# Attention norms with tokens on partitions, transposed back by DMA, in a linear-attention and PReLU feed-forward kernel

## The chip, the cores and the metric

The kernel runs on one core of a Trainium2 chip. The metric is the device time of one execution in microseconds, as the median of several runs. The core's engines work side by side, each through its own list of instructions in order: TensorE (PE; its weight loads are PEld), VectorE (DVE), ScalarE (ACT), GpSimd (POOL) and SyncE (SP). POOL and SP are used here almost only to issue DMAs: POOL the loads, SP the stores and the transposes.

## What is computed

There are 8 batches, 8 heads, 576 tokens and head dimension 64. Attention without a softmax is followed by an RMS norm over the head dimension and by a feed-forward layer with a parametric ReLU.

```python
kv = np.einsum('bhsd,bhse->bhde', k, v)
out = np.einsum('bhsd,bhde->bhse', q, kv)
rms = np.sqrt(np.mean(out * out, axis=-1, keepdims=True) + 1e-06)
attn = out / rms * g_norm                       # g_norm: 64 values
x = attn.transpose(0, 2, 1, 3).reshape(4608, 512)
h = x @ w_in                                    # 512 x 2048
g = np.maximum(h, 0.0) + alpha * np.minimum(h, 0.0)
y = g @ w_out                                   # 2048 x 512
```

Inputs and output are float32; the matmuls run in fp16 with float32 accumulation.

## The kernel before

The 4608 tokens are taken in nine windows of 512 (`W`). A batch has 576 tokens, so most windows hold the end of one batch and the start of the next. Heads are worked in four pairs, so that a pair fills 128 partitions.

**The feed-forward part.** For each window the hidden activations are made in 16 groups of 128 features. A group is `m1_group`: four matmuls of 512 columns (line 391) into a PSUM bank `h_ps`, then ACT makes `m_sb` = relu(-h) (line 398) and DVE combines both into `gt` (line 402), the fp16 activations. Two `m_sb` buffers are in use, and from window 2 on two PSUM banks for `h_ps` (`h_tags`). The second product of windows 1 to 8 is done by a Strassen-like scheme with seven products instead of eight, `prod_mm` (line 546), into three banks X, Y and Z; it needs sums of `gt` blocks (`s_sum`, DVE, lines 496 to 502) and reads of the banks (`y_read`: p1 and c11 on ACT, u2, u3, c22, c21 and c12 on DVE), after which rows are stored by SP. Window 0 takes the plain product (`y_mm`, line 416).

**The order** is written by hand. The main loop over `w` from 1 to 7 runs 16 units `u`. A unit issues group `u` of the first product of window `w`, then sums, then seven matmuls of the second product of window `w - 1` with its reads, and then a piece of the attention of window `w + 1`, by the tables `ATT_1` and `ATT_AT`. The last loop, over window 8's second product alone, has no attention and no first product.

**Attention.** For each pair: `step_t` (batches 0 to 2) turns q so that head dimension lies on partitions, with PE and a copy; from batch 3 (`B_NAT`) on `dma_t` does this with five DMA transposes on SP, all in unit 11. `step_kv` makes k^T v of a batch (five matmuls, line 327, and a DVE product with a block mask, line 335). `step_ot` multiplies it with the transposed q: `ot_ps` has the pair's features on partitions and 512 tokens as columns (line 349), and ACT squares it (line 355). `ssq_mm` sums the squares of a head over partitions by a matmul with a mask (line 365), and ACT makes `rstd` of it, 128 x 512 values (line 367). `norm` multiplies `ot_ps`, `g2col` (g_norm, one value a partition) and `rstd` into `xt` (DVE, line 375), the right-hand operand of the first product. No transpose of x is needed.

**Loads and buffers.** Weights stay in SBUF: `w_in_sb` in five parts, of 256, 256, 512, 512 and 512 features. k is regrouped by copies (DVE or ACT, `regroup`, lines 171 and 173). q has three buffers `qsb`, transposed q two (`qt_all`), and staging tiles two each. The pool for `ot_ps` has two banks.

Of the kernel before, what the change touches and what calls it, by code (L numbers as in the profile page):

```python
# [9 lines left out]
FP32 = mybir.dt.float32  # L10
# [7 lines left out]
def kernel(  # L18
# [29 lines left out]
    NC = D_MODEL // P  # L48
    assert NC == NPAIR and 0 < REM < P and P0 <= P and H % 4 == 0
    B_NAT = 3  # L50
    inv_d = 1.0 / D

    const_p = ctx.enter_context(tc.tile_pool(name="constp", bufs=1))
# [67 lines left out]
    bufs = []  # L121
    for i in range(NBUF):
        t = {}
        for nm in ("k", "v", "q"):
            n = 1 if nm == "v" else T0 if i == 0 else NT
            t[nm] = qkv_p.tile([P, n, H, D], FP16, name=f"{nm}sb{i}")
            if i > 0 or nm == "v":
                nc.vector.memset(t[nm][REM:P, n - 1, :, :], 0.0)
        bufs.append(t)
# [26 lines left out]
            )  # L156

    def buf_of(b, nm):
        return bufs[1 if nm == "q" and b >= B_NAT else b % NBUF][nm]

    def load_rem(b, nm):
        nc.gpsimd.dma_start(  # L162
# [2 lines left out]
        )  # L165

    def regroup(b, nm, h0, h1, eng=None):
        dst = bufs[b % NBUF][nm][:, 0:TPP, h0:h1, :].rearrange("p t h d -> p h t d")
        src = stages[b, nm][:, h0:h1, :, :]
        if eng is nc.scalar:  # L170
            nc.scalar.copy(out=dst, in_=src)
        else:
            (eng or nc.vector).tensor_copy(out=dst, in_=src)
# [35 lines left out]
    def load_w_in(i):  # L209
# [4 lines left out]
        )  # L214
        w_in_sb.append(t)

    def load_w_out(i):
        t = w_p.tile([P, GW, D_MODEL], FP16, name=f"w_out_sb{i}")
        nc.gpsimd.dma_start(
            out=t[:],  # L220
            in_=moe_w_out[i * GW * P : (i + 1) * GW * P, :].rearrange("(g p) m -> p g m", p=P),
        )
        w_out_sb.append(t)
# [25 lines left out]
    load_batch(1, ("v",))  # L249
    load_w_out(2)  # L250
    load_w_out(3)
    load_batch(2, ("q", "k", "v"))


    warm_ps = ps_q.tile([P, W], FP32, name="warm_ps", tag="q")
# [18 lines left out]
    def pair_cols(b, nm, j):  # L274
        def f(t):
            n = rows(b)
            if nm == "v" and b == 0:
                h = 2 * j % HH
                return stages[b, nm, 2 * j // HH][0:n, h : h + 2, t, :]
            if nm == "v" and t < TPP:  # L280
                return stages[b, nm][:, 2 * j : 2 * j + 2, t, :]
            if nm == "v":
                return bufs[b % NBUF][nm][0:n, 0, 2 * j : 2 * j + 2, :]
            return bufs[b % NBUF][nm][0:n, t, 2 * j : 2 * j + 2, :]
        return f

    def step_t(b, j, pool=(ps_s, "s")):
        qs = pair_cols(b, "q", j)
        qt_ps = pool[0].tile([P, n_runs(b) * rows(b)], FP16, name="qt_ps", tag=pool[1])
        c = 0  # L290
        for t in range(n_runs(b)):
            n = rows(b)
            nc.tensor.matmul(  # L293
                out=qt_ps[:, c : c + n],
                lhsT=qs(t),
                rhs=ident16[0:n, 0:n],
                is_transpose=True,
                start=(t == 0),
                stop=(t == n_runs(b) - 1),
            )  # L300
            c += n
        if j == 0:
            qt_all[b] = attn_p.tile([P, NPAIR, S], FP16, name="qt_all")
        qts[b, j] = qt_all[b][:, j, :]
        if b == 0 and j < 2:
            nc.vector.tensor_copy(out=qts[b, j], in_=qt_ps[:, 0:S])
        else:
            nc.scalar.copy(out=qts[b, j], in_=qt_ps[:, 0:S])

    qt_all = {}  # L310

    def dma_t(b):
        qt = attn_p.tile([P, NPAIR, S], FP16, name="qt_all")
        for t in range(NT):
            c0, c1 = t * P, min((t + 1) * P, S)
            src = stages[b, "q"][:, t] if t < TPP else buf_of(b, "q")[0:REM, TPP]
            nc.sync.dma_start_transpose(
                out=qt[:, :, c0:c1], in_=src.rearrange("p h d -> p (h d)"),
            )
        for j in range(NPAIR):  # L320
            qts[b, j] = qt[:, j, :]

    def step_kv(b, j, pool=(ps_s, "s")):
        ks, vs = pair_cols(b, "k", j), pair_cols(b, "v", j)
# [46 lines left out]

    def norm(w, j):
        ot_ps, rstd = ots.pop((w, j))
        xts[w, j] = xt_p.tile([P, W], FP16, name="xt", tag=f"xt{j}")
        nc.vector.scalar_tensor_tensor(  # L375
            out=xts[w, j][:], in0=ot_ps[:], scalar=g2col[:], in1=rstd[:],
            op0=ALU.mult, op1=ALU.mult,
        )

    gts = {}  # L380
# [8 lines left out]
    def m1_mm(h_ps, w, g, cs):  # L389
        for c in cs:  # L390
            nc.tensor.matmul(  # L391
                out=h_ps[:], lhsT=w_in_blk(c, g), rhs=xts[w, c][:],
                start=(c == 0), stop=(c == NC - 1),
            )

# [261 lines left out]
    ssq_mm(0, 2)  # L657
    keep_warm(1, warm_late)
    ssq_mm(0, 3, h_at(2))
    norm(0, 2)  # L660
    norm(0, 3)
    first = [ps_h.tile([P, W], FP32, name="h_ps", tag=f"h{g}") for g in range(3)]
    for c in range(3):
        for g in range(2):
            m1_mm(first[g], 0, g, (c,))
    m1_mm(first[2], 0, 2, (0, 1, 2))
    for g in range(3):
        m1_mm(first[g], 0, g, (3,))
        m1_evac(first[g], 0, g)
    h_turn[0] = 2  # L670
    for g in range(3, NF):
        m1_group(0, g, {3: S_POOL, 4: O_POOL, 5: O_POOL, 6: Q_POOL}.get(g))
        if g == 14:
            regroup(1, "k", 0, H)
            nc.vector.memset(bufs[0]["k"][REM:P, TPP, :, :], 0.0)


    ys = {}
# [82 lines left out]
            ATT_1.setdefault(at, []).append((what, j))  # L761
    ATT = {"t": step_t, "kv": step_kv, "ot": step_ot, "ssq": step_ssq}

    def attention(w, u):
        if w < NW:
            for what, j in (ATT_1 if w == 2 else ATT_AT).get(u, ()):
                if what == "t" and w >= B_NAT:
                    continue
                if w < B or what in ("ot", "ssq"):
                    if w == 2 and what in ("kv", "ssq"):  # L770
                        pool = Q_POOL if j % 2 == 0 else S_POOL
                        (step_kv if what == "kv" else step_ssq)(w, j, pool)
                    else:
                        ATT[what](w, j)

    REG_AT = {8 + 2 * j: (("k", j),) for j in range(NPAIR)}

    Y3_AT = [(8, 8), (8, 8), (8, 8), (8, 9), (9, 9), (9, 10), (10, 10), (10, 10), (10, 11), (11, 11), (11, 12), (12, 12), (12, 13), (13, 14), (14, 15), (15, 16)]
    REG_2 = {2 * j: (("k", j),) for j in range(NPAIR)}

    for w in range(1, NW):
        if w + 2 < B:
            load_gated(w + 2)
        for u in range(NF):
# [2 lines left out]
                unit_sums(w, u)  # L787
            if w == 1 and u == 2:
                regroup(2, "k", 0, H)
            if w == 1 and u == 3:  # L790
                dma_t(3)
            if w == 2 and u == 0:
                h_tags[0] = ("h1", "h2")
            if w > 2 and u == 0:
                y_read(w - 2, "c12")
            if w == 1:
# [4 lines left out]
            else:  # L801
                for i in range(u * PER, (u + 1) * PER):
                    prod_mm(w - 1, *Y_LIST[i])
                for what in Y_READS.get(u, ()):
                    y_read(w - 1, what)
            attention(w + 1, u)
            if w == 1:
                for k in {5: (0,), 7: (1,)}.get(u, ()):
                    s_sum(1, 1, k)
                    s_sum(1, 2, k)  # L810
            if w + 2 < B:
                for nm, j in REG_AT.get(u, ()) if w > 1 else ():
                    regroup_pair(w + 2, nm, j)
                if u == 11 and w > 1:
                    dma_t(w + 2)
            if w == 2:
                for nm, j in REG_2.get(u, ()):
# [51 lines left out]
```

## Time and profile before

Three runs took 283.4, 283.55 and 284.07 us; the median is 283.55. The profiled execution took 283.02 us, and its span from the first to the last instruction is 281.3 us. The clock granted to PE was 1.0 of full speed.

| Row of the profile | count | us each | us in all |
|---|---|---|---|
| first product, matmul, L391 | 576 | 0.379 | 145.4 |
| gt, DVE, L402 | 144 | 0.746 | 106.9 |
| m_sb, ACT, L398 | 144 | 0.598 | 85.9 |
| xt (norm), DVE, L375 | 36 | 0.744 | 26.6 |
| rstd, ACT, L367 | 36 | 0.689 | 24.6 |
| squares, ACT, L355 | 36 | 0.598 | 21.2 |
| sum of squares, matmul, L365 | 36 | 0.379 | 13.6 |
| ot, matmul, L349 | 64 | 0.286 | 13.6 |

The count is that of instructions. "us each" runs from start to end of one instruction; those of PE and also those of DVE and ACT overlap a little with their successors, so the pitch from start to start is shorter, and "us in all" counts overlapping time once. Group lines of the profile name the source line, the engine, the operation, output and inputs, and the idle time of the engine just before, with what ended it. Rows of busy times give a stretch in us from the span's start, its length, then the busy time and the count of instructions for PE, PEld, DVE, ACT and POOL, the PE clock, the share of DMA and GB/s.

### The profile page before, as it was taken

What the parts mean: (1) busy time and instruction counts of PE and PEld (TensorE: products, weight loads), DVE (VectorE), ACT (ScalarE), POOL (GpSimd) and SP (SyncE); (2) the same over time, 40 slices, a digit from 0 to 9 for tenths busy, and PEclk for the clock granted to TensorE, in tenths of its full rate; (3) what the DMA queues carried; (4) which work ended last, traced back from release to release, by engine and by line L of the source; (5) the groups of instructions that cost most, each with busy time, mean ns of one, the idle gap of its engine ahead of it and who ended that gap; (6) DMA issues with size and microseconds to landing.
All of it is one profiled execution on the core that took longest, in us unless ns stands there. A gap on an engine that the chain in (4) does not pass through costs nothing.

```text
span 281.3 us, 4978 instructions
## 1 busy us (share of the span) xinstructions
PE 273.9 (97%) x1888; PEld 173.6 (62%) x1888; DVE 219.8 (78%) x418; ACT 156.9 (56%) x268; POOL 61.8 (22%) x85
## 2 busy tenths in 40 slices
PE   7899999999999999999999999999999999999995
PEld 3444544554666676666666666666666666666784
DVE  6669729897778877887879787978887788787872
ACT  3567447697676645764576466645554566443310
POOL 8843333740630046006300450000000000000000
PEclk9999999999999999999999999999999999999999
DMA  8999999999794389946963698330112011201223
GB/s 164 198 207 195 198 201 193 192 136 143 100 170 85 93 84 150 165 112 115 158 102 97 121 150 123 93 106 1 40 37 75 2 37 37 77 0 37 77 76 114
DMA packets 77628, 31.37 MB, mean 112 GB/s; under 512 B 45780, under 2 KB 77284, under 8 KB 77604
## 3 DMA queue, kind: packets, MB, share of 16 engines
q0 software_dynamic: 55600, 18.85, 58.8%
q1 hardware_dynamic: 21108, 11.25, 16.1%
q10 hardware_dynamic: 896, 0.95, 1.0%
q8 instruction: 15, 0.25, 0.3%
q14 instruction: 9, 0.07, 0.1%
HBM read 36.71 MB, written 9.44 MB: 164 GB/s over the span
## 4 chain that ended last, share of the span: by engine, by line
PE 84%; DMA 10%; POOL 3%; issue 1%; DVE 1%; ACT 0%; DVEq 0%; POOLq 0%
PE h_ps L391 39%; PE yY L546 15%; PE yZ L546 10%; PE yX L546 10%; DMA vst<-in_v_dram 5%; DMA w_in_sb<-in_moe_w_in_dram 5%; PE kv_ps L327 3%; PE ot_ps L349 3%; PE ssq_ps L365 2%; PE y L416 2%; POOL w_in_sb L212 1%; POOL vst L136 1%; POOL kst L136 0%; PE qt_ps L293 0%; POOL qst L136 0%
## 5 line engine op out<-in xcount | busy, mean ns | idle before, releaser
L391 PE MATMUL h_ps<-xt,w_in_sb 128*128 128x512 f16 x576 | 145.4, 379 | 0.7 <-DVE gt L402 0.5
L402 DVE SCALAR_TENSOR_TENSOR gt<-m_sb,beta_sb,h_ps 128x512 f16<-128x512 f32 x144 | 106.9, 746 | 40.8 <-ACT m_sb L398 39.0
L398 ACT ACTIVATE m_sb<-h_ps 128x512 f32<-128x512 f32 x144 | 85.9, 598 | 75.8 <-PE h_ps L391 61.1
L391 PEld LDWEIGHTS <-w_in_sb 128*128 128x128 f16 x576 | 54.8, 98 | 47.0 <-issue 1.7
L546 PEld LDWEIGHTS <-s 128*128 128x128 f16 x512 | 50.1, 98 | 19.3
L546 PEld LDWEIGHTS <-gt 128*128 128x128 f16 x384 | 37.6, 98 | 15.1 <-issue 0.4
L546 PE MATMUL yY<-wsum,s 128*128 128x256 f16 x256 | 36.3, 273 | 0.0
L546 PE MATMUL yX<-w_out_sb,gt 128*128 128x256 f16 x256 | 35.1, 273 | 0.1
L355 ACT ACTIVATE sq_sb<-ot_ps 128x512 f16<-128x512 f32 x36 | 21.2, 598 | 16.5 <-PE ot_ps L349 16.4
L367 ACT ACTIVATE rstd<-ssq_ps,eps_t 128x512 f32<-128x512 f32 x36 | 24.6, 689 | 9.7 <-PE ssq_ps L365 9.2
L375 DVE SCALAR_TENSOR_TENSOR xt<-ot_ps,g2col,rstd 128x512 f16<-128x512 f32 x36 | 26.6, 744 | 3.2 <-ACT rstd L367 3.2
L162 POOL DMA_DIRECT2D qsb<-in_q_dram x7 | 4.9, 695 | 79.1 <-DMA qt_all<-qsb 77.0
L153 POOL DMA_DIRECT2D qst<-in_q_dram x20 | 17.7, 920 | 1.9 <-DVE gt L402 1.9
L546 PE MATMUL yZ<-w_out_sb,s 128*128 128x256 f16 x128 | 17.6, 273 | 0.0
L546 PE MATMUL yZ<-wsum,s 128*128 128x256 f16 x128 | 17.6, 273 | 0.0
L546 PE MATMUL yY<-wsum,gt 128*128 128x256 f16 x128 | 17.6, 273 | 0.0
L416 PE MATMUL y<-w_out_sb,gt 128*128 128x512 f16 x64 | 17.0, 379 | 0.5 <-DMA w_out_sb<-in_moe_w_out_dram 0.5
L349 PE MATMUL ot_ps<-qt_all,kv_sb 128*128 128x512 f16 (+7 forms) x64 | 13.6, 286 | 0.4 <-DVE kv_sb L335 0.3
L498 DVE TENSOR_TENSOR s<-s,gt 128x512 f16<-128x512 f16 x32 | 13.5, 421 | 0.5
L327 PEld LDWEIGHTS <-ksb 128*128 128x128 f16 (+1 forms) x164 | 11.4, 98 | 3.7 <-DVE ksb L193 1.1
L365 PE MATMUL ssq_ps<-sq_sb,mask 128*128 128x512 f16 x36 | 13.6, 379 | 0.1
L335 DVE TENSOR_TENSOR kv_sb<-kv_ps,mask 128x128 f16<-128x128 f32 x32 | 9.1, 286 | 5.5 <-PE kv_ps L327 5.5
(66 smaller groups left out, 210.1 us busy)
## 6 DMA issues: line engine op xcount, KB each, us to landing
out_dram<-y_sb SPq DMA_DIRECT2D x19, 256.0 KB, 2.2
kst<-in_k_dram POOLq DMA_DIRECT2D x7, 512.0 KB, 8.6
vst<-in_v_dram POOLq DMA_DIRECT2D x7, 512.0 KB, 11.0
qst<-in_q_dram POOLq DMA_DIRECT2D x20, 128.0 KB, 6.8
w_out_sb<-in_moe_w_out_dram POOLq DMA_DIRECT2D x4, 512.0 KB, 16.0
out_dram<-y_sb SPq DMA_DIRECT2D x25, 64.0 KB, 3.5
w_in_sb<-in_moe_w_in_dram POOLq DMA_DIRECT2D x3, 512.0 KB, 11.3
out_dram<-y_sb SPq DMA_DIRECT2D x9, 128.0 KB, 2.1
```

Of the source, the lines that this page charges most:

```text
L153: nc.gpsimd.dma_start(out=st[:, t, :, :], in_=srcs["q"][b, :, t * P : (t + 1) * P, :].rearrange("h p d -> p h d"),)
L327: nc.tensor.matmul(out=kv_ps[:], lhsT=ks(t), rhs=vs(t), start=(t == 0), stop=(t == n_runs(b) - 1),)
L349: nc.tensor.matmul(out=ot_ps[:, n0 - w * W : n1 - w * W], lhsT=kvs[b, j][:], rhs=qts[b, j][:, n0 - b * S : n1 - b * S], start=True, stop=True,
L355: nc.scalar.activation(out=sq[:], in_=ot_ps[:], func=AF.Square)
L365: nc.tensor.matmul(out=ssq_ps[:], lhsT=mask16[:], rhs=sq[:], start=True, stop=True)
L367: nc.scalar.activation(out=rstd[:], in_=ssq_ps[:], func=AF.Abs_reciprocal_sqrt, bias=eps_t[:], scale=inv_d,)
L375: nc.vector.scalar_tensor_tensor(out=xts[w, j][:], in0=ot_ps[:], scalar=g2col[:], in1=rstd[:], op0=ALU.mult, op1=ALU.mult,)
L391: nc.tensor.matmul(out=h_ps[:], lhsT=w_in_blk(c, g), rhs=xts[w, c][:], start=(c == 0), stop=(c == NC - 1),)
L398: nc.scalar.activation(out=m_sb[:], in_=h_ps[:], func=AF.Relu, scale=-1.0)
L402: nc.vector.scalar_tensor_tensor(out=gts[w, i][:, r, :], in0=m_sb[:], scalar=beta_sb[:, g : g + 1], in1=h_ps[:], op0=ALU.mult, op1=ALU.add,)
L416: nc.tensor.matmul(out=y[:], lhsT=gt_cols(w, g, a * P, (a + 1) * P), rhs=w_out_blk(g), start=(g == 0), stop=(g == NF - 1),)
L546: nc.tensor.matmul(out=bank, lhsT=lhs, rhs=rhs, start=fresh, stop=(c == NK - 1), skip_group_check=True,)
```

## The change

From window 4 on (`W_ROW`) attention is made with tokens on partitions. `rows_mm` takes 128 tokens at a time: the transposed q is the stationary operand and k^T v the moving one, a 128-column matmul for each pair, into one bank of 128 tokens x 512 features. Where the 128 tokens straddle two batches, two matmuls add up, each with 64 columns of zeros beside its q; for this the transposed q lies in two fixed tiles `qt_sb` with zeroed pads. ACT squares the bank, DVE sums the squares of each head by a reduce along the free dimension (128 x 8 results), ACT makes `rstd_r` of these, and DVE multiplies the bank by `rstd_r`, broadcast along the head, into `x_rows`. A DMA transpose on SP then writes these 128 tokens into `xt`, now one tile for all four pairs. `ssq_mm` and `norm` stay for windows 0 to 3.

g_norm is no longer part of the norm: the five parts of `w_in_sb` are multiplied by `g2col` in place on DVE in the stage of window 0. From batch 5 on the transposes of q are issued in portions in units 9, 10 and 11; those of batch 3 move from unit 3 to unit 12 of the loop over window 1, those of batch 4 from unit 11 to unit 12. q has two buffers instead of three. k^T v of windows 4 to 7 moves to units 0 to 3. Two entries of `Y3_AT`, which places the last row block of window 0's second product, and a bank turn at the start of window 2 change too.

```diff
-        for nm in ("k", "v", "q"):
+        for nm in ("k", "v", "q") if i < 2 else ("k", "v"):
...
     def buf_of(b, nm):
-        return bufs[1 if nm == "q" and b >= B_NAT else b % NBUF][nm]
+        return bufs[min(b, B_NAT) % 2 if nm == "q" else b % NBUF][nm]
...
+    def scale_w_in(i):
+        nc.vector.tensor_scalar(
+            out=w_in_sb[i][:], in0=w_in_sb[i][:], scalar1=g2col[:], scalar2=None, op0=ALU.mult,
+        )
...
+    PAD = P // 2
+    qt_sb = [const_p.tile([P, NPAIR, PAD + S + PAD], FP16, name=f"qt_sb{i}") for i in range(2)]
+
+    def dma_t(b, ts=tuple(range(NT))):
+        qt = qt_sb[b % 2][:, :, PAD : PAD + S]
+        for t in ts:
...
     def norm(w, j):
         ot_ps, rstd = ots.pop((w, j))
-        xts[w, j] = xt_p.tile([P, W], FP16, name="xt", tag=f"xt{j}")
-        nc.vector.scalar_tensor_tensor(
-            out=xts[w, j][:], in0=ot_ps[:], scalar=g2col[:], in1=rstd[:],
-            op0=ALU.mult, op1=ALU.mult,
+        nc.vector.tensor_mul(out=xt_cols(w, j), in0=ot_ps[:], in1=rstd[:])
...
+    def rows_mm(w, i):
+        n0 = w * W + i * P
+        b, r = divmod(n0, S)
+        o_ps = ps_o.tile([P, W], FP32, name="or_ps", tag="o")
+        for j in range(NPAIR):
+            cols = o_ps[:, j * P : (j + 1) * P]
+            if r + P <= S:
+                c = PAD + r
+                nc.tensor.matmul(
+                    out=cols, lhsT=qt_sb[b % 2][:, j, c : c + P], rhs=kvs[b, j][:],
+                    start=True, stop=True,
+                )
+            else:
...
+        sq = attn_p.tile([P, W], FP16, name="sq_sb")
+        nc.scalar.activation(out=sq[:], in_=o_ps[:], func=AF.Square)
+        ots[w, "r", i] = (o_ps, sq)
+
+    def rows_ssq(w, i):
+        o_ps, sq = ots.pop((w, "r", i))
+        ssq = attn_p.tile([P, H], FP32, name="ssq_r")
+        nc.vector.tensor_reduce(
+            out=ssq[:], in_=sq[:].rearrange("p (h d) -> p h d", h=H),
+            axis=mybir.AxisListType.X, op=ALU.add,
+        )
+        rstd = attn_p.tile([P, H], FP32, name="rstd_r")
+        nc.scalar.activation(
+            out=rstd[:], in_=ssq[:], func=AF.Abs_reciprocal_sqrt, bias=eps_t[:], scale=inv_d,
+        )
+        ots[w, "r", i] = (o_ps, rstd)
+
+    def rows_norm(w, i):
+        o_ps, rstd = ots.pop((w, "r", i))
+        xr = attn_p.tile([P, H, D], FP16, name="x_rows")
+        nc.vector.tensor_tensor(
+            out=xr[:], in0=o_ps[:].rearrange("p (h d) -> p h d", h=H),
+            in1=rstd[:].unsqueeze(2).to_broadcast([P, H, D]), op=ALU.mult,
+        )
+        xt_cols(w, 0)
+        nc.sync.dma_start_transpose(
+            out=xts[w][:, :, i * P : (i + 1) * P], in_=xr[:].rearrange("p h d -> p (h d)"),
+        )
...
+    scale_w_in(0)
     norm(0, 2)
     norm(0, 3)
...
+    scale_w_in(1)
     m1_mm(first[2], 0, 2, (0, 1, 2))
...
+    SCALE_AT = {3: 2, 7: 3, 11: 4}
     h_turn[0] = 2
     for g in range(3, NF):
+        if g in SCALE_AT:
+            scale_w_in(SCALE_AT[g])
         m1_group(0, g, {3: S_POOL, 4: O_POOL, 5: O_POOL, 6: Q_POOL}.get(g))
         if g == 14:
             regroup(1, "k", 0, H)
-            nc.vector.memset(bufs[0]["k"][REM:P, TPP, :, :], 0.0)
+            for nm in ("k", "q"):
+                nc.vector.memset(bufs[0][nm][REM:P, TPP, :, :], 0.0)
+            for t in qt_sb:
+                nc.vector.memset(t[:, :, 0:PAD], 0.0)
+                nc.vector.memset(t[:, :, PAD + S : PAD + S + PAD], 0.0)
...
+    ATT_ROW = {}
+    for what, ats in (("kv", (0, 1, 2, 3)), ("mm", (4, 6, 8, 10)), ("ssq", (5, 7, 9, 11)), ("norm", (6, 8, 10, 12))):
+        for j, at in enumerate(ats):
+            ATT_ROW.setdefault(at, []).append((what, j))
+    ROWS = {"kv": step_kv, "mm": rows_mm, "ssq": rows_ssq, "norm": rows_norm}
+    QT_AT = {9: (0, 1), 10: (2,), 11: (3, 4)}
+
     def attention(w, u):
-        if w < NW:
+        if W_ROW <= w < NW:
+            for what, j in ATT_ROW.get(u, ()):
+                if what != "kv" or w < B:
+                    ROWS[what](w, j)
+            if w + 1 < B:
+                dma_t(w + 1, QT_AT.get(u, ()))
+        elif w < NW:
...
-            if w == 1 and u == 3:
-                dma_t(3)
             if w == 2 and u == 0:
                 h_tags[0] = ("h1", "h2")
+                h_turn[0] = 1
...
+            if w == 1 and u == 12:
+                dma_t(3)
...
-                if u == 11 and w > 1:
+                if u == 12 and 1 < w < W_ROW - 1:
                     dma_t(w + 2)
```

## The prediction

> **What bounds the kernel now.** I read the page first (busy shares, clock, chain), then a window's row of busy times, then the timelines of TensorE, VectorE (DVE) and ScalarE (ACT) over one window, then the start, and last the tile of the transposed q for its DMAs.
>
> ```profile
> PE 273.9 (97%) x1888; PEld 173.6 (62%) x1888; DVE 219.8 (78%) x418; ACT 156.9 (56%) x268; POOL 61.8 (22%) x85
> PE 84%; DMA 10%; POOL 3%; issue 1%; DVE 1%; ACT 0%; DVEq 0%; POOLq 0%
> 155.70:184.60 28.90, 28.90 (x211) 19.34 (x209) 23.65 (x45) 17.38 (x31) 7.33 (x9) 1.00 0.89 121
> ```
>
> TensorE bounds it: the chain runs through PE for 84%, and in a window of 28.90 us PE is busy for 28.90. So PE work that goes is worth its full length, if nothing else becomes late. Within one unit of that window:
>
> ```profile
> 162.68 0.39 PE L327 MATMUL kv_ps<-vst,ksb 128*128 128x128 f16 x4
> 162.91 0.22 PE L327 MATMUL kv_ps<-vsb,ksb 128*128 128x128 f16 x1
> 162.96 1.03 PE L391 MATMUL h_ps<-xt,w_in_sb 128*128 128x512 f16 x4
> 163.83 0.93 PE L546 MATMUL yX<-w_out_sb,gt 128*128 128x256 f16 x7
> 164.59 0.38 PE L365 MATMUL ssq_ps<-sq_sb,mask 128*128 128x512 f16 x1
> 164.81 1.03 PE L391 MATMUL h_ps<-xt,w_in_sb 128*128 128x512 f16 x4
> ...
> 164.03 0.60 ACT L398 ACTIVATE m_sb<-h_ps 128x512 f32<-128x512 f32 x1 [1.31 <-DVE kv_sb L335]
> 165.01 0.69 ACT L367 ACTIVATE rstd<-ssq_ps,eps_t 128x512 f32<-128x512 f32 x1 [0.38 <-PE ssq_ps L365]
> 165.87 0.60 ACT L398 ACTIVATE m_sb<-h_ps 128x512 f32<-128x512 f32 x1 [0.18 <-PE h_ps L391]
> ...
> 164.66 0.75 DVE L402 SCALAR_TENSOR_TENSOR gt<-m_sb,beta_sb,h_ps 128x512 f16<-128x512 f32 x1 [0.62 <-ACT m_sb L398]
> 165.32 0.68 DVE L568 TENSOR_TENSOR u<-yY,p 128x512 f32<-128x512 f32 x1
> 165.92 0.74 DVE L375 SCALAR_TENSOR_TENSOR xt<-ot_ps,g2col,rstd 128x512 f16<-128x512 f32 x1
> 166.58 0.74 DVE L402 SCALAR_TENSOR_TENSOR gt<-m_sb,beta_sb,h_ps 128x512 f16<-128x512 f32 x1
> ```
>
> Starts give the real pitches. PE: a 512-column matmul 0.216 us, five 128-column ones 162.68 to 162.96, so 0.056 each, seven of the second product 0.76; a bare unit is 0.87 + 0.76 = 1.63. The third group is ACT, the fourth DVE. From the start of a group (162.96) it is 1.07 us to m_sb and 1.70 to gt. A group may only start when gt of two groups before has left its bank (two banks), 2.50 us after that group started (1.70 + 0.75 + 0.05); two units are 3.26 or more. So DVE may run about 0.8 us late, no more. On ACT, rstd waits for PE only, so the next m_sb is never held by DVE. That is what changes.
>
> [...] No reduce is in this trace; the 128x2048 fp16 copy[...] took 686. [...] the trace has 685 for `u`. [...] the trace has 689 for rstd at N = 512[...].
>
> **The change, part by part.**
>
> *PE work, windows 4 to 8.* Per window go four ssq matmuls (4 x 0.216) and the ot ones (4 x 0.22): 1.74. Sixteen 128-column matmuls come: 16 x 0.056 = 0.90. That saves 0.84 a window, 4.2 in five; windows 5 and 7 have a block that straddles two batches (4 more each, 0.45 in all): 3.8 saved.
>
> *DVE and ACT, same windows.* In the built order, at units 5, 7, 9 and 11 DVE has gt(u), the other sums of that unit, then the reduce; ACT has m_sb(u), then rstd_r, which waits for that reduce, then m_sb(u+1); and the next thing in DVE's list is gt(u+1), which waits for m_sb(u+1). So DVE idles through reduce -> rstd_r -> m_sb -> gt, four times a window. From the reduce's start to gt(u+1): reduce 0.69[...], hand-over DVE to ACT 0.09 (at 19.27 m_sb follows a gt that ended at 19.18), rstd_r 0.28 - 0.09 = 0.19[...], m_sb to gt 0.63 (164.03 to 164.66): 1.60.
>
> Now DVE in order, from the start of group 5 as 0, with pitches from the timeline: gt 0.66, u and c reads 0.60, x_rows 0.60 (a PSUM tensor_tensor like `u`), sums 0.34 (0.45 before a dependent one). gt(5) 1.70; u2 2.36; reduce 2.96; gt(6) 4.56; two sums 5.22; x_rows 6.01; gt(7) 6.61; sum 7.27; reduce 7.61; gt(8) 9.21; sum 9.87; x_rows 10.21; gt(9) 10.81; sum 11.47; u3 11.81; reduce 12.41; gt(10) 14.01; sum 14.67; x_rows 15.01; gt(11) 15.61; sum 16.27; c22 16.61; reduce 17.21; gt(12) 18.81; sum 19.47; x_rows 19.81, done 20.50.
>
> PE needs gt(u) + 0.80 for group u+2: group 8 at 5.36 (0.25 late), 9 at 7.41 (0.20), 10 at 10.01 (0.97), 11 in time, 12 at 14.81 (1.32), 13 in time, 14 at 19.61 (1.54). Together 4.28 a window; without lateness group 14 would start at 9 x 1.63 + 3 x 0.22 = 15.33. Five windows: 21.4.
>
> *SP and the transposes of x.*
>
> ```profile
> L317 SPq DMA_TRANSPOSE qt_all<-qst x20: 1191/1217/1840, 62.9 to 182.0; - x20
> DMA to landing us min/median/max: 2.3/2.3/7.1
> ```
>
> One transpose holds SP for about 1.25 us with its gap and lands 2.3 after issue. The last x_rows is done at 20.50, the next window's first group is due at 19.61 + 2 x 1.63 = 22.87 and needs all four transposes. With SP free, 20.55 + 2.3 is just in time. In the loops over windows 3 to 5, SP works through what was queued ahead: third x transpose 15.75, one of q, the c22 store (0.5), two of q, so the last is issued about 21.4 and lands about 23.7: 0.8 late, three times, 2.4. Bounds: 0, and 4.8 more each if the 7.1 us landing is met. Stores behind them have four y buffers: nothing waits. The q portions' loads are in long before; POOL's order of loads is unchanged, and moving block 3's transposes to unit 12 costs nothing, since before they only started at 62.9, when q had landed.
>
> *w_in scaled in window 0.* DVE row of the start:
>
> ```profile
> 15.50 1.41 DVE L375 SCALAR_TENSOR_TENSOR xt<-ot_ps,g2col,rstd 128x512 f16<-128x512 f32 x2 [1.11 <-ACT rstd L367]
> 18.43 7.29 DVE L402 SCALAR_TENSOR_TENSOR gt<-m_sb,beta_sb,h_ps 128x512 f16<-128x512 f32 x10 [1.52 <-ACT m_sb L398]
> ```
>
> The first scaling fits the 1.11 idle. The second follows the norms (done about 17.2), where group 2 would start at 16.44: gt(0) moves by 0.5, to 18.95. The third stands behind gt(2) (pitch 0.73: 20.4, free 21.1) and takes 0.69: group 4, which waits for it, starts at 21.85. Before it started at 19.1 (m_sb of group 10 at 25.36, less 1.07, less 6 x 0.864): +2.75. The fourth stands behind gt(6): from group 4, 2 x 0.864 + 1.70 + 0.66 + 0.69 + 0.05 = 4.83, where four groups take 3.45: +1.38; the fifth the same. Sum 5.5.[...] Five more memsets (0.27 for q's buffer, four pads of about 0.2 by the 0.17 to 0.27 of the ones in the trace: 1.1 us) stand before gt(15), so that the fourth row block of y, which takes its bank, waits 0.75. Two DMA waits of PE in this stretch (0.46 and 0.38) go, as the data are there by then. Net +5.4.
>
> *At nothing:* the norm without g (0.06 x 16 on DVE, under PE), the merged xt tile, kv in units 0 to 3 (0.1 at one of them).
>
> **Sum.** 283.02 (the profiled execution; span 281.3, 1.7 around it; median of the runs 283.55) + 21.4 + 2.4 + 5.4 - 3.8 = 308.4. I say 308.
>
> **Rivals.**
> 1. *The PE saving decides* (the faster side): DVE finds cover for reduces and scalings, and 3.8 us go: 279.2. For it: DVE is idle for a fifth of the window, and adding 4 x (0.6 + 0.6 - 0.66) = 2.2 leaves it under 28. Against: the idle time lies between gt and m_sb, and the new chain uses it up in order. It decides if reduce to gt took under 0.55 instead of 1.60 (20 bubbles), and w_in were scaled ahead of need.
> 2. *Only window 0 pays:* 283.0 + 5.4 - 3.8 = 284.6. For it: the scaling is as certain as anything here; against, as in 1.
> 3. *Half of the window loss:* the reduce at 0.53, rstd_r at 0.1 and some sums out of the way: 1.35 instead of 1.60 takes 1.0 a window away and the transposes' lateness: 301; with more cover still, 290 to 300.
> 4. *The transposes queue up* (over 4 us to land): 312 to 318.
>
> **How the numbers follow.** Forecast, 301 to 313: 0.70. Rival 3 under 301: 0.11. Rival 4: 0.07. Rival 2: 0.04. Rival 1: 0.08. What can be told from no change is about 0.3%, 0.9 us. Range 296 to 314; it leaves out rivals 1 and 2, the lower part of 3 and the upper of 4. Faster 0.08, same 0.02, slower 0.90.
>
> **What would show it.** Right: PE below 0.9 busy in the slices of windows 4 to 8, the PE wait for DVE gt (0.5 us now) grown to some 20; ACT rstd_r waiting for the DVE reduce, 20 times; a loop over windows 3 to 5 near 33 us instead of 28.9; PE waiting for w_in from DVE three times before 35 us. Wrong: windows near 28.1 with PE full, or a reduce far under 0.5.

## The result, and the profile after

The changed kernel took 312.97 us in the median of four runs (312.39 to 314.14), beside 283.48 (283.1 to 284.07) for the kernel before on the same chip: 1.105 times as long, with a 95% interval of 1.102 to 1.108. The forecast was 308, with a range of 296 to 314; the median lies near its upper end. The profiled execution took 314.14 us with a span of 312.2, so 30.9 more than the span before.

From the page of the changed kernel: busy time of each engine, two rows of the span in 40 slices, and the chain of what ended last.

```profile
PE 277.1 (89%) x1920; PEld 173.3 (55%) x1920; DVE 231.7 (74%) x447; ACT 144.2 (46%) x268; POOL 61.8 (20%) x85
...
PE   7868899998999998779977898689888987899995
...
PEclk9998999999999999999999999999999999999999
...
PE 66%; DMA 13%; DVE 11%; ACT 4%; issue 2%; POOL 2%; ACTq 0%; DVEq 0%; POOLq 0%
```

PE was busy for 97% of the span; now it is for 89%. The row of slices shows where it went: a 6 at the start, then nearly full slices, then 7s and 8s and a 6 among the 9s from slice 16 to 35 (a slice is 7.8 us), which are the loops over windows 3 to 7, in which attention for windows 4 to 8 is made. The share of PE in the chain fell from 84% to 66%; DVE (1% to 11%), ACT (0% to 4%) and DMA (10% to 13%) took it.

From the waits of the changed kernel (what waited, for what; us in all, times, longest):

```profile
ACT rstd_r L419 <- DVE ssq_r L414: 48.9, 20, 3.1
...
PE h_ps L447 <- DVE gt L458: 15.8, 16, 1.3
...
PE h_ps L447 <- DMA xt<-x_rows: 5.6, 4, 2.0
PE h_ps L447 <- DVE w_in_sb L219: 5.5, 4, 2.3
```

PE's three waits in these lines are 26.9 us, of a loss of 30.9. On ACT, rstd_r waits 20 times for the reduce, once for each block of rows; on PE, the first product waits for gt in the same windows, for the transposes of x at four loop starts, and for the scaled weights at the start.

The chain that the prediction worked out, seen in the loop over window 4 (timeline of DVE and ACT; start, length, what it waited for in brackets):

```profile
150.98 0.68 DVE L414 TENSOR_REDUCE ssq_r<-sq_sb 128x8 f32<-128x512 f16 x1
...
151.69 0.30 ACT L419 ACTIVATE rstd_r<-ssq_r,eps_t 128x8 f32<-128x8 f32 x1 [2.01 <-DVE ssq_r L414]
151.90 0.58 ACT L454 ACTIVATE m_sb<-h_ps 128x512 f32<-128x512 f32 x1
...
152.51 0.75 DVE L458 SCALAR_TENSOR_TENSOR gt<-m_sb,beta_sb,h_ps 128x512 f16<-128x512 f32 x1 [0.85 <-ACT m_sb L454]
```

ACT stands for 2.01 us in front of rstd_r. For the last 1.0 of these the next group's m_sb could have run behind it, since the matmuls that it reads ended at 150.68; then m_sb runs, and only then can DVE go on with gt. From the start of the reduce to the start of gt it is 1.53 us, four times a window.

The timeline of PE at the start, the first three of its waits for scaled weights:

```profile
17.63 2.33 PE L447 MATMUL h_ps<-xt,w_in_sb 128*128 128x512 f16 x10 [0.40 <-DVE w_in_sb L219]
22.30 5.21 PE L447 MATMUL h_ps<-xt,w_in_sb 128*128 128x512 f16 x16 [2.34 <-DVE w_in_sb L219]
28.79 3.63 PE L447 MATMUL h_ps<-xt,w_in_sb 128*128 128x512 f16 x16 [1.27 <-DVE w_in_sb L219]
```

Sixteen matmuls take 5.21 us after the second wait and 3.63 after the third. The windows of the same stretch say why (us; busy time and count for PE, PEld, DVE, ACT, POOL; then the granted clock):

```profile
22.30:25.00 2.70, 2.70 (x7) 1.04 (x8) 0.74 (x2) 0.60 (x1) 0.81 (x1) 0.50 1.52 192
25.00:28.80 3.80, 2.53 (x12) 0.85 (x10) 2.83 (x5) 1.79 (x3) 1.55 (x3) 0.93 1.41 198
```

The clock is 0.50 in the first 2.7 us after the wait of 2.34 and, by the 0.93 of the next row, for some 0.5 us more. The sixteen matmuls lose 1.6 us by it, which no step of the prediction had.

To compare kernels I read two times off each PE timeline: when the first product of loop 2 (the loop over window 2) starts, and how long it is from there to the start of the last group of the first product. The first holds the start, the second the loops.

| Kernel | time (one profiled execution) | loop 2 starts at | from there to the last group |
|---|---|---|---|
| before | 283.02 | 66.51 | 197.50 |
| after | 314.14 | 72.80 | 221.93 |
| 1: rstd behind the next m_sb | 301.06 | 71.62 | 210.03 |
| 2: q transposes behind those of x | 306.28 | 70.66 | 216.21 |
| 3: no scaling of w_in | 310.39 | 66.02 | 224.96 |
| 3b: no scaling, q of batch 3 loaded last | 305.90 | 66.03 | 220.59 |
| 4: no row windows | 290.43 | 73.91 | 197.51 |
| 5: short reduce | 309.55 | 72.81 | 217.32 |
| 6: 2 and 5 together | 300.17 | 73.09 | 207.66 |
| 7a: 1, 2 and early scaling | 290.44 | 66.96 | 204.09 |
| 7b: 7a, rows and q transposes two units earlier | 291.28 | 66.78 | 205.09 |
| 8: 7b, four x_rows buffers and more | 280.70 | 66.53 | 194.89 |

So of the 30.9 us, 6.3 are lost before loop 2, 24.4 in the loops and 0.2 after them. The row of 7b is one of its three slower executions (291.28 to 295.13 us, with a granted clock of 0.987 to 0.994); the other three, at about 1.0, have a median of 287.43.

The times also hold what PE's clock did. Wherever it fell before PE's last matmul, it stayed at 0.50 for some 3.4 us (read from rows of busy times over 0.2 us each; in the changed kernel from 22.14 to 25.55). Such a stretch costs up to 1.7 us, as an estimate from these two numbers: half its length. It fell once at the start in the changed kernel and in 4, 5 and 6, and in the loops twice in 1, once in 3 and in 7b, and for 6.8 and 3.4 us in 5. It did not fall in the kernel before, in 2, 3b, 7a and 8. The mean granted clock goes with this: 0.995 in the changed kernel, 0.994 in 4, 6 and 7b, 0.993 in 3, 0.988 in 1 and 0.976 in 5, and at least 0.998 in the others. Experiments 1 to 6 are single executions, so a difference of 2 or 3 us between them can be the clock's alone.

### The profile page after: what moved, and what is told of

Read it like the earlier page. It is cut to its first block, busy times and chain, and to the rows that moved or that the text cites. A ratio compares the mean times of both kernels' runs of the same rounds, so it can differ in the third digit from the quotient of the medians.

```text
span 312.2 us, 5142 instructions
## 1 busy us (share of the span) xinstructions
PE 277.1 (89%) x1920; PEld 173.3 (55%) x1920; DVE 231.7 (74%) x447; ACT 144.2 (46%) x268; POOL 61.8 (20%) x85
## 4 chain that ended last, share of the span: by engine, by line
PE 66%; DMA 13%; DVE 11%; ACT 4%; issue 2%; POOL 2%; ACTq 0%; DVEq 0%; POOLq 0%
PE h_ps L447 31%; PE yY L602 12%; PE yX L602 8%; DMA vst<-in_v_dram 6%; DMA xt<-x_rows 6%; DVE gt L458 6%; PE yZ L602 5%; ACT m_sb L454 4%; PE y L472 3%; PE kv_ps L331 3%; PE or_ps L393 1%; POOL qst L154 1%; DVE x_rows L427 1%; PE ot_ps L353 1%; DVE w_in_sb L219 1%
## 5 line engine op out<-in xcount | busy, mean ns | idle before, releaser
L447 PE MATMUL h_ps<-xt,w_in_sb 128*128 128x512 f16 x576 | 147.3, 382 | 27.3 <-DVE gt L458 15.8
L447 PEld LDWEIGHTS <-w_in_sb 128*128 128x128 f16 x576 | 54.1, 98 | 77.3 <-issue 27.5
L602 PEld LDWEIGHTS <-gt 128*128 128x128 f16 x384 | 37.5, 98 | 14.9
L419 ACT ACTIVATE rstd_r<-ssq_r,eps_t 128x8 f32<-128x8 f32 x20 | 6.0, 301 | 48.9 <-DVE ssq_r L414 48.9
L427 DVE TENSOR_TENSOR x_rows<-or_ps,rstd_r 128x512 f16<-128x512 f32 x20 | 13.7, 684 | 0.5 <-DMA xt<-x_rows 0.5
L331 PE MATMUL kv_ps<-vst,ksb 128*128 128x128 f16 (+1 forms) x136 | 12.6, 219 | 1.6 <-DMA vst<-in_v_dram 1.4
L414 DVE TENSOR_REDUCE ssq_r<-sq_sb 128x8 f32<-128x512 f16 x20 | 13.6, 678 | 0.0
L552 DVE TENSOR_TENSOR s<-gt 128x512 f16<-128x512 f16 x32 | 13.3, 419 | 0.1
## 6 DMA issues: line engine op xcount, KB each, us to landing
w_out_sb<-in_moe_w_out_dram POOLq DMA_DIRECT2D x4, 512.0 KB, 15.8
```

Of the source, the lines that this page charges most:

```text
L331: nc.tensor.matmul(out=kv_ps[:], lhsT=ks(t), rhs=vs(t), start=(t == 0), stop=(t == n_runs(b) - 1),)
L414: nc.vector.tensor_reduce(out=ssq[:], in_=sq[:].rearrange("p (h d) -> p h d", h=H), axis=mybir.AxisListType.X, op=ALU.add,)
L427: nc.vector.tensor_tensor(out=xr[:], in0=o_ps[:].rearrange("p (h d) -> p h d", h=H), in1=rstd[:].unsqueeze(2).to_broadcast([P, H, D]), op= ...
L447: nc.tensor.matmul(out=h_ps[:], lhsT=w_in_blk(c, g), rhs=xts[w][:, c, :], start=(c == 0), stop=(c == NC - 1),)
L552: nc.vector.tensor_add(out=t[:], in0=a21, in1=a22)
L602: nc.tensor.matmul(out=bank, lhsT=lhs, rhs=rhs, start=fresh, stop=(c == NK - 1), skip_group_check=True,)
```

## The experiments

Theory A is the prediction's: DVE and ACT wait for each other in their orders (reduce, rstd_r, m_sb, gt), and that, not the amount of work, makes PE wait. Theory SP: the transposes of x come late because q's stand ahead of them in SP's list. The rivals were that the duration of the work on DVE decides, and that the start pays for most of it. Beside the experiments the kernel before took 283.31, 283.37 and 283.33 us.

**1. rstd_r issued behind the next group's m_sb.** The computation is the same.

```diff
+        ots[w, "r", i] = (o_ps, ssq)
+
+    def rows_rstd(w, i):
+        o_ps, ssq = ots.pop((w, "r", i))
         rstd = attn_p.tile([P, H], FP32, name="rstd_r")
...
-    for what, ats in (("kv", (0, 1, 2, 3)), ("mm", (4, 6, 8, 10)), ("ssq", (5, 7, 9, 11)), ("norm", (6, 8, 10, 12))):
+    for what, ats in (("rstd", (6, 8, 10, 12)), ("kv", (0, 1, 2, 3)), ("mm", (4, 6, 8, 10)), ("ssq", (5, 7, 9, 11)), ("norm", (6, 8, 10, 12))):
```

> Only change to the changed kernel: rstd_r of a row block is issued on ScalarE after the next unit's m_sb instead of before it; same instructions, same count. Theory A (the hand-over reduce, rstd_r, m_sb, gt stalls VectorE in order): from the reduce's start to the next gt 0.6 us instead of 1.53, 20 times, so some 3.7 us a window off VectorE's list; most of PE's 15.8 us of waits for gt goes; about 296 us (293 to 300). Theory B (VectorE simply has too much work with reduce and x_rows): the list is no shorter, within 3 us of 313. Theory C (the DMA transposes of x are the main cost): also within 3 us of 313, and the PE waits for xt stay near 5.6.

301.06 us. The timeline of DVE and ACT around one reduce:

```profile
181.79 0.67 DVE L414 TENSOR_REDUCE ssq_r<-sq_sb 128x8 f32<-128x512 f16 x1
182.39 0.73 DVE L462 SCALAR_TENSOR_TENSOR gt<-m_sb,beta_sb,h_ps 128x512 f16<-128x512 f32 x1
```

gt now follows the reduce at once, 0.60 after its start instead of 1.53. PE's wait for gt fell from 15.8 to 2.6 us. So the chain is shown to be the cause of these waits, with no work taken away. But the gain stopped 5 us short of the expected 296. The waits of this kernel, and the row of PE's clock from its page:

```profile
PE h_ps L451 <- DMA xt<-x_rows: 7.8, 4, 2.6
PE h_ps L451 <- DVE gt L462: 2.6, 5, 1.3
...
PEclk9999999999999999997999799999999999999999
```

The wait for the transposes of x grew from 5.6 to 7.8: the loops became shorter, and the transposes did not come earlier by as much. After the two longest of these waits (2.55 and 2.35 us, before loops 4 and 5) the clock fell to half, the two 7s of the row, which is worth up to 3.4 us more.

**2. q's transposes behind those of x.**

```diff
-    QT_AT = {9: (0, 1), 10: (2,), 11: (3, 4)}
+    QT_AT = {13: (0, 1), 14: (2,), 15: (3, 4)}
```

> Only change: the five transposes of q are issued in units 13 to 15, behind all four of x, instead of 9 to 11. Theory A with SP's queue as a second cost: the waits of the first group of a window for xt fall in the loops over windows 3, 4 and 5 (1.8, 2.0 and 1.2 us now) to about the 0.8 that the loop over window 7 has without q transposes; 309 to 311 us. Theory C (transposes dominate): 304 or less. If the landing itself is late whatever stands ahead of it: no change, 313.

306.28 us, 3 to 5 better than expected, though not the 304 of theory C. The wait for xt fell from 5.6 to 0.8 us and that for gt stayed at 15.8, as SP had it. By the table 5.7 us were won in the loops. Another 2.1 lie before loop 2, which the edit doesn't touch: in this run the wait of 2.31 us for the weights was followed by sixteen matmuls in 3.63 us, at full clock.

**3. No scaling of w_in.** This leaves out the multiplication by g_norm.

```diff
-    scale_w_in(0)
...
-    scale_w_in(1)
...
-        if g in SCALE_AT:
-            scale_w_in(SCALE_AT[g])
```

> Leaves out the five multiplications of w_in by g_norm, so g_norm is not applied at all; everything else as in the changed kernel. If the waits for the scaled w_in and the halved PE clock after the longest of them make the start late: the loop over window 1 starts about 6.2 us earlier (0.5 of the 7.15 is gt of group 15 behind the memsets), 306 to 307 us, and the PE clock stays at 1.0 from 20 to 29 us. If the data would be late anyway, as w_in's loads: less than 2 us.

310.39 us: a miss. Loop 2 starts at 66.02, so the start is regained in full, 6.8 us; but loop 2 then takes 35.57 us, where it takes 29.75 in the kernel before. Of these 5.8 us, 4.0 are one wait in PE's timeline, and behind it the clock was at half from 75.6 to 79.0, worth some 1.7 more:

```profile
74.28 0.38 PE L331 MATMUL kv_ps<-vst,ksb 128*128 128x128 f16 x4 [3.97 <-DMA vst<-in_v_dram]
```

v of batch 3 is issued at 58.99, within half a microsecond of when it was before, and takes 15.2 us to land instead of 11.4. On SP, in this kernel and below in the kernel before:

```profile
56.73 8.01 SPq L321 DMA_TRANSPOSE qt_sb<-qst  x4
```

```profile
62.92 5.37 SPq L317 DMA_TRANSPOSE qt_all<-qst  x4
```

Before, the transposes of q of batch 3 began 4.4 us behind the load of v; here they begin 2.3 ahead of it and run beside it. In the changed kernel they begin 1.4 ahead (62.42 and 63.80), v takes 14.3 us, and PE waits 1.0 for it. That gave theory T.

**3b. As 3, with q of batch 3 loaded behind its v**, so that its transposes can't run beside that load.

```diff
-        if b == B_NAT:
-            load_q(b)
         load_rem(b, "k")
...
         load_main(b, "v")
+        if b == B_NAT:
+            load_q(b)
```

> Leaves out the scaling of w_in by g_norm, as the third experiment did, and loads q of batch 3 after its v instead of ahead of its k. Theory T (the q transposes of batch 3 no longer wait for the old buffer, start 6 us earlier and run beside the load of v, which then lands late): v lands in about 10 us instead of 15.2, kv of batch 3 waits for it less than 1 us instead of 3.97, and the time is 306 to 307.5. Theory L (the load of v is late for another reason, such as the weights' loads or chance): the wait stays above 3 and the time at 310. If q itself is then late, the wait shows at the first product of loop 2 or at ot of batch 3 as a wait for qt_sb.

305.90 us. v of batch 3 took 8.8 us to land, q's transposes start at 65.03, behind it, and PE's wait for v is 0.4. Loop 2 takes 29.76 again. That is as T has it. The landing of this load goes with the start of the transposes: 15.2 us where they begin 2.3 ahead of it, 14.3 at 1.4 ahead, 11.4 at 4.4 behind, 8.8 with none beside it. Against the 312.97 of the changed kernel the run is 7.1 us faster, of which 6.8 lie at the start; in loop 2 the wait of 1.0 for v has gone too. Note what happened in 3: work was taken away, an engine came free, transfers started earlier, and they collided with others.

**4. No row windows**, with the scaling and the new q buffers kept.

```diff
-    W_ROW = 4
+    W_ROW = 9
```

> Only change: no window takes the row path (it would start at window 9, and there are windows 0 to 8); w_in scaled, buffers, moved transposes as in the changed kernel. Computes the same. If the row windows cost 23 and the start 7: 290 to 291 us, windows of 28.9 us with PE full. If the merged xt tile, the two q buffers or the moved transposes of blocks 3 and 4 had a cost of their own, it would show here as more than 292.

290.43 us, as expected. The loops take 197.51 us, those before 197.50. All that is left, 7.1 us, is the start (7.4 by the table, 1.0 of it a wait for v at 8.2 us that is 0.4 in the changed kernel). So the cost of the change is two separate things, 7 at the start and the rest in the row windows.

**5. A reduce over 8 of the 64 elements of a head.** This leaves out 7/8 of the squares.

```diff
-            out=ssq[:], in_=sq[:].rearrange("p (h d) -> p h d", h=H),
+            out=ssq[:], in_=sq[:].rearrange("p (h d) -> p h d", h=H)[:, :, 0:8],
```

> Leaves out 7/8 of the squares: the reduce sums only 8 of the 64 of each head, so that it takes some 0.2 instead of 0.68 us; the wait for rstd_r stays as it is. Theory A (the sum of VectorE's work between two gt decides, reduce, hand-over and wait together): each of the 20 reduces gives its 0.48 us back wherever VectorE is late, at most 9.6 us in all, less where a group had slack: 303 to 306 us, PE's wait for gt from 15.8 to 6 to 9. Theory W (the engines' waiting on each other decides, the reduce itself lies in idle time): 310 us or more, the wait for gt above 13.

309.55 us, which is between the two. (In this expectation and the next, A stands for the whole way from reduce to gt, with the reduce itself.) The reduce takes 0.21 us instead of 0.68, and the wait for gt fell from 15.8 to 7.8, inside A's 6 to 9. The time did not follow: the wait for xt rose to 7.5 us, its longest to 3.15, and after the two longest (3.15 and 2.21) PE's clock fell again (after the first, four matmuls took 1.86 us instead of 1.02). By the lengths of these stretches, less 0.9 us in which PE stood anyway, the clock cost some 4.7 us in the loops; without it the run would be at about 305, inside A's 303 to 306. That is an estimate. Alone, this run settles nothing about the time; it called for the next.

**6. The short reduce with the order of experiment 2.** It leaves out the same squares.

```diff
-            out=ssq[:], in_=sq[:].rearrange("p (h d) -> p h d", h=H),
+            out=ssq[:], in_=sq[:].rearrange("p (h d) -> p h d", h=H)[:, :, 0:8],
...
-    QT_AT = {9: (0, 1), 10: (2,), 11: (3, 4)}
+    QT_AT = {13: (0, 1), 14: (2,), 15: (3, 4)}
```

> Leaves out 7/8 of the squares in the reduce, as the short reduce did, and puts the q transposes behind the x transposes, as experiment 2 did. Theory A+SP (the short reduce gave its 8 us of waits for gt back, and lost them again because the x transposes kept their own timetable and PE's clock fell after the longer waits for xt): with the transposes out of the way the two gains add: 306.3 minus 7 to 8, 298 to 300 us, waits for xt below 2 us. Rival (the reduce's duration is worth little by itself): 304 or more.

300.17 us, at the upper end of what A and SP together have. In the loops it is 8.6 us below experiment 2, for 20 x 0.47 = 9.4 us of reduce taken away: once the transposes no longer hide it, a microsecond on that chain is worth nearly one of the total. The two losses are in series here: the earlier one hides part of the next.

**7a and 7b. A kernel without the three losses.** 7a joins 1 and 2, scales the third part of the weights right behind the second and the last two four groups earlier, and moves the memsets out of the first product of window 0. 7b has, besides, each row piece and q's transposes two units earlier, possible since the first two blocks need only batches whose kv is ready.

```diff
     scale_w_in(1)
+    scale_w_in(2)
...
-    SCALE_AT = {3: 2, 7: 3, 11: 4}
+    SCALE_AT = {3: 3, 7: 4}
...
-    for what, ats in (("rstd", (6, 8, 10, 12)), ("kv", (0, 1, 2, 3)), ("mm", (4, 6, 8, 10)), ("ssq", (5, 7, 9, 11)), ("norm", (6, 8, 10, 12))):
+    for what, ats in (("rstd", (4, 6, 8, 10)), ("kv", (0, 1, 2, 3)), ("mm", (2, 4, 6, 8)), ("ssq", (3, 5, 7, 9)), ("norm", (4, 6, 8, 10))):
...
-    QT_AT = {9: (0, 1), 10: (2,), 11: (3, 4)}
+    QT_AT = {11: (0, 1), 12: (2,), 13: (3, 4)}
```

The scalings are those of both kernels, the last two pairs of lines those of 7b.

> The change with rstd_r issued behind the next group's m_sb (experiment 1), the q transposes behind the x transposes (experiment 2), and the scalings put as early as their loads land, with the memsets moved off the path of gt(15). Theory A with the measured terms: 283.5, minus 3.8 of PE work, plus about 1.5 of the start left, plus 2.6 of gt waits, plus 1 to 2 for xt: 284 to 287 us. Rival (the losses are not additive: with the DVE chain gone, the x transposes are late by as much, or PE's clock drops at the loop starts): 290 or more.

> As the combined kernel, with each piece of the row windows two units earlier (products at units 2, 4, 6, 8; reduce at 3, 5, 7, 9; rstd and norm at 4, 6, 8, 10) and the q transposes at units 11 to 13. Theory A: the x transposes land before the next loop begins, so no wait for xt: 281.5 to 284 us, that is from 2 us below the kernel before to equal. Rival (the x transposes are late whatever the unit, since the queue or the DMA engines are taken by others): no difference from the combined kernel.

7a: 289.39 us (288.88 to 290.44), ratio 1.022 (1.019 to 1.024), 2.4 us over the upper end of A's and nearer to its rival. 7b: 287.43 us, ratio 1.015 (1.012 to 1.019), a miss of A's 281.5 to 284 as well. The start is back (66.96 and 66.78), and in 7b no wait of PE for xt is left. A new wait had come instead, of PE for gt (5.4 us in 7a, 8.2 in the 7b of the table), seen in 7a on SP, DVE and PE:

```profile
114.00 1.20 SPq L439 DMA_TRANSPOSE xt<-x_rows  x1
...
122.76 0.69 DVE L434 TENSOR_TENSOR x_rows<-or_ps,rstd_r 128x512 f16<-128x512 f32 x1 [2.08 <-DMA xt<-x_rows]
...
124.16 1.02 PE L454 MATMUL h_ps<-xt,w_in_sb 128*128 128x512 f16 x4 [1.98 <-DVE gt L465]
```

and, from the view of the tile x_rows over the same stretch:

```profile
DMA to landing us min/median/max: 2.4/4.4/8.7
```

There are two x_rows buffers. The transpose issued at 114.00, while a batch was being loaded (POOL issued its loads from 104.84 to 112.2), landed 8.7 us later and kept its buffer till then; the third norm waited for it on DVE, and gt waited behind the norm. In the changed kernel, whose blocks come further apart, this wait was 0.5 us in all.

**8. Four x_rows buffers**, the two more in the memory of `rstd`, which the row windows don't use; q of batch 3 loaded behind v, as in 3b; the last two weight parts scaled a group's columns at a time, one ahead of each gt.

```diff
+        if i % 2:
+            xr = attn_p.tile([P, 2 * H, D], FP16, name="x_rows", tag="rstd")[:, 0:H]
+        else:
+            xr = attn_p.tile([P, H, D], FP16, name="x_rows")
...
-        if g in SCALE_AT:
-            scale_w_in(SCALE_AT[g])
+        if g + 4 in range(8, NF):
+            scale_w_in((g + 4) // 4 + 1, g % 4)
```

> The kernel of experiment 7b (rows two units earlier) with four x_rows buffers instead of two (so that VectorE's third and fourth norm no longer wait for the transpose that reads the buffer two before: 2.8 us at 120.9 there), q of batch 3 loaded behind its v, and the scalings of the last two weight parts in pieces of one group's columns, one ahead of each gt. Theory A (every loss of the change is one of the four waits found, and the work saved on PE is worth about 4 us): waits for gt below 2 us in all, for v below 0.5, start within 1 us of before: 279.5 to 282.5, so faster than before. Rival (the x transposes' holds on the DMA queue come through somewhere else, for instance at the loop starts): 284 or more.

280.84 us (280.33 to 281.2), ratio 0.991, interval 0.990 to 0.992: inside A's range and 2.5 us below the kernel before. Its page and its waits:

```profile
PE 271.5 (97%) x1920; PEld 174.0 (62%) x1920; DVE 230.2 (83%) x453; ACT 147.5 (53%) x268; POOL 62.1 (22%) x85
...
PE   7898999999999999999999999999999999999994
```

```profile
PE h_ps L458 <- DVE gt L469: 1.1, 3, 0.8
PE h_ps L458 <- DVE w_in_sb L220: 0.4, 1, 0.4
```

DVE does as much as in the changed kernel (230.2 beside 231.7 us) and hinders nobody. The amount of work on DVE was not the problem. What each of the three edits of this kernel is worth was not separated.

## Why the prediction was right

The direction, the mechanism and the size came out: 312.97 against a forecast of 308, inside the range. By its terms:

**The chain on DVE, 21.4 us: confirmed.** The predicted times, counted from the start of group 5, can be laid beside the loop over window 4. Reduce to gt: 1.60 predicted, 1.53 measured. The reduce took 0.68 for 0.69; rstd_r began 0.03 behind its end for 0.09, and took 0.30 for 0.28; m_sb began 0.21 behind the start of rstd_r for 0.19, and gt 0.61 behind that of m_sb for 0.63. The 0.69, 0.28 and 0.19 were my estimates, shown by nothing in the trace of the kernel before, which has no reduce and no ACTIVATE of 8 elements; nearest to the reduce is `u`, 685 ns for 512 elements. PE's waits in that loop after group 5, which started at 148.02 (timeline of PE):

```profile
157.89 1.02 PE L447 MATMUL h_ps<-xt,w_in_sb 128*128 128x512 f16 x4 [0.71 <-DVE gt L458]
162.60 1.02 PE L447 MATMUL h_ps<-xt,w_in_sb 128*128 128x512 f16 x4 [1.08 <-DVE gt L458]
167.33 1.02 PE L447 MATMUL h_ps<-xt,w_in_sb 128*128 128x512 f16 x4 [1.30 <-DVE gt L458]
```

These are groups 10, 12 and 14, at 9.87, 14.58 and 19.31 after group 5; predicted were 10.01, 14.81 and 19.61. At 8 and 9, where 0.25 and 0.20 were foretold, no wait is listed, but the starts, 5.29 and 7.36, are near the predicted 5.36 and 7.41. In the kernel of experiment 8, which has the same products and nearly no waits, group 14 comes at 15.42 (163.02 to 178.44 in the loop over window 5), so a window loses 3.9 where 4.28 were predicted, about 19.5 in five if all are like this one. Experiment 1 shows the order to be the cause, experiment 6 that the duration counts too. The reduce took 678 ns for 512 elements a partition and, in experiment 5, 209 for 64: 1.05 ns for each element more, as an estimate from these two.

**Transposes, 2.4 us: mechanism right, too small.** The order on SP was as worked out (in loop 4 an x transpose, two of q, x, one of q, a store, two of q, x), and the last x was late behind the loops over windows 3 to 5. But PE waited 1.78, 1.95 and 1.16 us there instead of 0.8 each, and 0.75 behind the loop over window 7, where nothing was predicted; behind 6 nothing, as predicted. In the loop over window 4 the last one goes out at 170.21, 22.2 us after group 5, where 21.4 was the estimate: the third x transpose held SP for 2.04 us instead of 1.2.

```profile
163.52 2.04 SPq L432 DMA_TRANSPOSE xt<-x_rows  x1
```

The bounds, 0 and 4.8 a window, did hold it. Experiment 2 wins 5.7 us, which is this term as measured. The prediction's fourth rival, transposes that queue up, is thus part of the truth, and the 312.97 lies in its range (312 to 318) too. But its sign, over 4 us to land, is not what made the loops late: the last x transposes, for which they waited, landed 2.4 us after their issue (3.1 behind the loop over window 7), and it was the issue that came late.

**Scaling of w_in, 5.4 us: the waits right, one effect missing.** The first, short stall was 0.40 for 0.5, the three others 2.34, 1.27 and 1.45 for 2.75, 1.38 and 1.38; the wait of y was 0.46 for 0.75. The scaling of 2048 elements took 0.74 to 0.93 us where the prediction has 0.69, which is what the fp16 copy of 2048 elements takes in the kernel before (686 to 688 ns); DVE was otherwise as assumed. The 1.6 us of half clock came on top; altogether the scaling costs 7.1 (experiments 3b and 4).

**PE work saved, 3.8 us: right in kind, smaller.** It can't be seen in the changed kernel. With the waits gone, in experiment 8, the stretch from loop 2 on is 2.6 us shorter than before. The blocks of four row products take 0.22 us each, as predicted; PE has no idle time over 0.2 there, and where the other 1.2 us stayed was not tested.

Sum of the measured terms: 283.0 + 19.5 + 5.7 + 7.1 - 2.6 = 312.7, against the 314.1 profiled. The rest, 1.4, isn't assigned. Against the predicted 308.4 the chain was 1.9 too high and the other three terms and this rest together 7.6 too low. So the number came closer than its terms, because part of their errors cancelled.

**Why not the rivals.** Rivals 1 and 2 are excluded as descriptions of this kernel by the wait for gt, 15.8 us. Rival 3 supposed a reduce of 0.53 us and an rstd_r of 0.1, without a trace that showed either; 0.68 was measured, and 0.21 from rstd_r to m_sb. But rival 1 named the two conditions under which the saving decides, a short way from reduce to gt and scaling ahead of need. Experiment 8 comes near to the first (0.60 from reduce to gt, seen in experiment 1) and meets the second, and needed two more that rival 1 did not name: x transposes ahead of q's with some units to spare, and enough x_rows buffers. It reaches 280.84 where rival 1 said 279.2.

## What to carry to other kernels

When a statistic goes from one engine to another and back inside a loop where both run in order, put the second engine's piece behind its next piece of loop work: the same work then took 12 us less here (experiment 1). Removing a stall makes the next one visible, so expect part of a gain back (in experiments 3, 5 and 7a transfers or buffers came due that had been covered) and read the waits again each time. Weights could be scaled in place here nearly for nothing (loop 2 of experiment 8 starts at 66.53, before at 66.51), when each piece is scaled as it lands and well before its product, in pieces that fit the slack of the scaling engine.

## What the hardware showed that I had not expected

**PE's clock fell to half after some waits of 2.2 us and more, for 3.4 us, and on a beat.** The first product's third weight part came late in six kernels by nearly the same time. PE's timeline in experiment 1 and in experiment 4:

```profile
22.68 3.63 PE L451 MATMUL h_ps<-xt,w_in_sb 128*128 128x512 f16 x16 [2.41 <-DVE w_in_sb L219]
```

```profile
23.29 5.31 PE L447 MATMUL h_ps<-xt,w_in_sb 128*128 128x512 f16 x16 [2.33 <-DVE w_in_sb L219]
```

After waits of 2.31 to 2.56 us in six kernels the same sixteen matmuls took 3.63 us twice and 5.21 to 5.31 four times. Of the waits in the loops, those of 2.21 to 3.97 us were followed by half clock in six cases of seven, those up to 2.04 never. So the length of the wait alone does not decide. The row of experiment 5's page shows three falls:

```profile
PEclk9997999999999999987999799999999999999999
```

They begin at 22.9, 135.6 and 173.1 (rows of busy times over 0.2 us each). The distances, 112.7 and 37.5 us, are 33 and 11 times 3.41, and the stretches at half clock last 3.4, 6.8 and 3.4. In experiment 1 they begin at 134.7 and 168.8, 34.1 or 10 times 3.41 apart, and once more at 298.5, after PE's last matmul, 129.7 or 38 times 3.41 later. So in these two runs the falls lay on a beat of 3.41 us, which lay differently in each. In all ten cases where the clock fell while PE had work left, PE had been idle for 2.1 us or more of the 3.41 us before the fall (in the changed kernel 2.2, from 19.96 to 22.14).

Three long waits had no fall behind them: 2.41 us in experiment 1, 2.31 in 2 and 2.37 in 3b. In experiment 1 the beat, counted back from 134.7, cuts the wait into 1.8 and 0.6. In 2 and 3b the clock fell only once, at the end (303.25 and 303.16); if the beat holds there too, which these two runs don't show, it cuts the waits into 0.4 and 1.9 and into 0.6 and 1.8. That is an estimate, open by up to some 0.3 us where it counts many beats back (over 80 in 2). So what went with a fall may be how much of a wait lay within one beat; how much it takes is not shown, since 1.9 and 2.1 are nearer to each other than the estimate is exact.

**A DMA transpose between two tiles in SBUF lands 2.4 us after its issue, or 8.** In the changed kernel the transposes of x took 2.4 us to land in the median and 8.6 at most. In 7a six took 5.4 to 8.7 us, and each of these went out within 9 us after a batch's loads had been issued. The disturbance seems to go both ways: v of batch 3 landed in 8.8 us with no transposes of q beside it and in 11.4 to 15.2 with them. Experiment 3b moved q's load together with its transposes, so it fits a collision of the two without showing which resource they share.
